# Where the bounds of q and k are formed, and how one planner prices its DMA queue: block-causal attention with a feed-forward layer

## The chip, the cores and the metric

The kernel runs on one core of one Trainium2 chip. The metric is the device time in microseconds. A core has TensorE (PE: matmuls, and weight loads shown as PEld), VectorE (DVE), ScalarE (ACT), GpSimd (POOL) and SyncE (SP), which here issues every load, store and DMA transpose from one queue in program order. Each engine runs its own instructions in the order in which they were written, and waits on semaphores for the others.

## The reference

```python
B, H, S, D = 8, 8, 576, 64
scores = (q @ k^T) / sqrt(D)              # mask: key block j <= query block i, blocks of 64
attn = exp(scores - rowmax); attn = attn / (sum(attn) + 1e-9)
x = (attn @ v) laid out as (B*S, H*D)     # 4608 tokens of 512
h = x @ w_in                              # 512 x 2048
g = h * clip(h + 3, 0, 6) / 6
out = g @ w_out                           # 2048 x 512, f32
```

All inputs and the output are f32.

## The kernel before

**Number format.** Most products are done in f16 with each operand split into a high and a low part (hi = round(a * scale), lo = a * scale - hi), and the partial products are summed in PSUM. The scale is a power of two, taken from an upper bound of the operand: `pow2_scale` sums a per-partition bound over the 128 partitions with a matmul by ones (tile `mb_q`), clears the mantissa (`pw_q`), divides and inverts (`rs_q`).

**Work units.** Heads are taken in pairs: 4 pairs for each of 8 batches, so 32 slots. The first batch (slots 0 to 3) is done in f32 by `qk_load32`, `qk_prep32`, `s_block32`, `t_block32` and `pv_group32`, so that it can start before any scale is known. Slots 4 to 31 are done in f16: `qk_load` (two DMA loads into `qk`), `qk_prep` (bound, scale, split into `qks`, DMA transpose into `qkT`), `s_group` (scores into PSUM tile `s`, row maxima, exp into `p`, normalised and split into `phl`, DMA transpose into `pT`), `pv_group` (attention times v, into the feed-forward's input `x`). The feed-forward goes over 13 pieces of up to 384 tokens; for each of 16 strips of 128 hidden columns `ffn1` makes `h`, ACT makes `r` = relu, DVE and ACT make `g`, and `ffn2` accumulates `o`. PSUM holds three `s` tiles, two `h` tiles and three `o` tiles. The weights are loaded, turned into f32 words and split during the first 180 us (`rawi`, `rawo`, `sgi`, `exi`, `win`, `wout`, and the bounds `abi`, `abo`, which ACT forms by Abs with a running sum).

**The order of the work** is not written by hand. A `Recorder` collects every operation with its operands, and `schedule` then plays them through a model of five engines: `cost` gives each instruction's time on its engine and its latency, and at each step an engine takes the ready operation with the lowest due time (`key`). The due times come from the constants at the top of the file: `AS`, `U`, `TA`, `PV0` for the f32 start, `RT` for the rest of batch 0, the table `AT` for slot starts, `FT` for the feed-forward, `S0`, `W0`, `M0` for the weights, `QL` for how many slot lengths ahead the loads of q and k are keyed. An operation added by `nc.scaled(..., "AV")` may go to ACT or DVE, whichever the model thinks ends first, with a bias against DVE; "P" adds POOL. The order that results is fixed for each engine when the program is built; on the chip only the waits move. In this model a DMA transpose has a fixed latency that does not depend on what else is in flight, and loads share a second, simple model of a queue.

**What the change touches.** In `qk_prep`, line 762 (`absmax(mx, t)`): one VectorE reduction with absolute values over 2 x 576 columns gives the bound of q and of k for each partition (tile `qkmx`). In `pv_group32`, lines 947 and 948: three small products on POOL fill `rd`, a diagonal of reciprocal row sums, which a matmul (tile `pr`) spreads for the f32 start, 12 times 3. In `s_group`, line 1033: VectorE multiplies the negated row maxima `st` by the scale `esc`, giving the bias of the exp. In `Recorder`: the pricing of DMAs at lines 208 to 218 and 423 to 426, and when a consumer counts as ready at line 438. Lines 26 to 53 and 81 hold the constants. `qks` has one buffer, `qk` two.

In the profile every recorded operation carries the line of `emit` (L452), so the groups are told apart by their tiles.

Of the kernel before, what the change touches and what calls it, by code (L numbers as in the profile page):

```python
# [9 lines left out]
BF16 = mybir.dt.bfloat16  # L10
# [3 lines left out]
AF = mybir.ActivationFunctionType  # L14
# [8 lines left out]
WX = 10  # L23
WY = 27

U = 2.788
AS = (7.494, 11.408, 15.3, 22.633)
AL = 14.807
PV0 = 2.519
TA, TR, PR = 2.197, 5.661, 0.677  # L30
QR = 3.417
PVA, PVB = 0.93, 1.25
PHS = 18
WLP = 0
WHA = 0
# [5 lines left out]
MEM = 0  # L41

NMIN = 64
QL = 0.849
VL = 0.2
W0, WD = 4.938, 2.891
S0, SD = 57.576, 4.59
M0, MD = 34.073, 5
RT = (25.619, 42.369, 59.881, 71.242)
RS, RL, VL1 = 2.796, 15.216, 24.0  # L50
VM0, VMX = 10.452, 0.3
AT = ((4, 86.25), (6, 128.63), (8, 159.32), (10, 199.92), (12, 240.31), (14, 287.79), (16, 335.13), (24, 565.96), (32, 826.62))
FT = ((0, 28), (1, 100), (2, 168.81), (3, 239.13), (4, 279.57), (5, 356.87), (7, 505.16), (10, 740.96), (13, 988.23))
QP = 0.55
VP = 0.5
BLK = 64
# [4 lines left out]
class Op:  # L61

    __slots__ = ("ways", "key", "preds", "joint", "n", "start", "end", "tiles", "eng", "half")


class Engine:
# [9 lines left out]
        return call  # L78


ADV = {("tensor", "a"): 60.0}


class Recorder:
# [3 lines left out]

    NAMES = ("tensor", "vector", "scalar", "gpsimd", "sync")
    LAT = {"tensor": 55, "vector": 37, "scalar": 39, "gpsimd": 65, "sync": 65}  # L90
    TURN = 95
    BIAS = {"vector": 250.0, "gpsimd": 500.0}
    EDGE = 0.0
# [66 lines left out]
    def add(self, ways):  # L160
        eng, method, args, kw = ways[0]
        outs, ins = self.operands(args, kw)
        last = self.ops[-1] if self.ops else None
        if eng == "tensor" and self.joint is not None and last and last.joint == self.joint:
            op = last
            calls, occ, _, _ = op.ways[eng]
            more, took, _ = self.cost(eng, method, args, kw, outs, ins)
            op.ways[eng] = (calls + [(method, args, kw)], occ + more, occ + took, False)
        else:
            op = Op()  # L170
            op.joint, op.n, op.ways = None, len(self.ops), {}
            for e, m, a, k in ways:
                op.ways[e] = ([(m, a, k)], *self.cost(e, m, a, k, *self.operands(a, k)))
            op.key = self.key - self.adv.get((eng, self.cls), 0.0)
            op.preds, op.tiles, op.start = {}, [], None
            op.half = eng == "tensor" and outs[0].ap[0][1] <= 64 and method == "matmul"
            if eng == "tensor":
                op.joint = self.joint
            self.ops.append(op)
        for a, w in [(a, False) for a in ins] + [(a, True) for a in outs]:  # L180
            if self.on_chip(a):
                self.touch(op, a, w)

    def touch(self, op, a, w):
# [17 lines left out]
        keep.append((op, w, p0, p1, b0, b1))  # L202
        self.hist[t.name] = keep

    def cost(self, eng, method, args, kw, outs, ins):


        n = self.count(outs[0])
        if method == "dma_start":
            nb = mybir.dt.size(outs[0].dtype)  # L210
            for _, c in list(outs[0].ap):
                nb *= c
            if kw.get("transpose"):
                occ = max(1290, 172 * nb / 32768 - 150)
                return occ, occ + (1100 if nb <= 4 * 32768 else 2100), False
            if eng == "gpsimd":
                return 1300, 2900 + nb / 170, False
            return 600, 2000 + nb / 170, False
        if eng == "vector":
            if method == "tensor_reduce":  # L220
                n = self.count(ins[0])
            else:
                ptr = any(isinstance(a, bass.AP) and self.count(a) == 1 for a in args[2:] if n > 1)
                ptr = ptr or n == 1 and method == "tensor_scalar_mul" and isinstance(args[2], bass.AP)
            wide = [a for a in ins if self.count(a) > 1 and not self.psum(a)]
            port = len(wide) > 1
            if method in ("tensor_scalar", "tensor_copy") and n > 1:
                if not any(self.psum(a) for a in outs + ins):
                    if len(outs[0].ap) == 2 or outs[0].ap[1][1] % 2 == 0:
                        n = n / (4 if mybir.dt.size(outs[0].dtype) + mybir.dt.size(ins[0].dtype) == 4 else 2)  # L230
                        port = True
            occ = 68 + 1.042 * n
            if method != "tensor_reduce" and ptr:
                occ += 57
            return occ, occ + 80, port
        if eng == "scalar":
            occ = 94 + 0.8335 * n
            if isinstance(kw.get("scale"), bass.AP):
                occ += 95
            if isinstance(kw.get("bias"), bass.AP):  # L240
                occ += 58
            if "accum_out" in kw:
                occ += 93
            return occ, occ + 105, False
        if eng == "gpsimd":
            if method == "memset":
                return 20 + 1.0 * n, 50 + n, False
            occ = 75 + (2.0 if method == "tensor_tensor" else 1.1) * n
            return occ, occ + 30, True
        f32 = mybir.dt.size(ins[0].dtype) == 4  # L250
        occ = max(n / 2.37, 26) * (4 if f32 else 1) + 2
        if f32 and method == "matmul":
            occ = max(occ, 200)
        if method == "transpose":
            occ = max(occ / 2, 100)
        if outs[0].ap[0][1] <= 64 and method == "matmul":
            occ = occ / 2
        return occ, occ + 172, False

    def schedule(self):  # L260
# [63 lines left out]
        while done < N:  # L324
# [95 lines left out]
            o.eng, o.start, o.end = e, t, t + took  # L420
            while head < N and ops[head].start is not None:
                head += 1
            if calls[0][0] == "dma_start" and not calls[0][2].get("transpose"):
                nb = (took - (2900.0 if e == "gpsimd" else 2000.0)) * 0.8
                dma = max(dma, o.end - nb - 400.0) + nb
                o.end = max(o.end, dma + 400.0)
            now[e] = t + occ
            self.busy[e] += occ
            for x in o.tiles:
# [5 lines left out]
            for s, flow in succ[pick]:  # L435
                rs = ready[s]
                for q in rs:
                    r = t if q == e and (e == "tensor" or not flow) else o.end + self.LAT[q]
                    rs[q] = max(rs[q], r)
                ndep[s] -= 1  # L440
                if not ndep[s]:
                    for q in rs:
                        heapq.heappush(pend[q], (rs[q], s))
# [12 lines left out]
def kernel(  # L456
# [92 lines left out]
    def absmax(o, i, axis=AX.XY):  # L549
        nc.vector.tensor_reduce(o, i, axis=axis, op=ALU.max, apply_absolute_value=True)  # L550
# [207 lines left out]
    def qk_prep(n):  # L758
        t = qn.pop(n)
        mx = sm.tile([P, 2], F32, tag="qkmx", name=f"qkmx{n}")  # L760
        sp = attp.tile([P, 3, NST, 2, D], F16, tag="qks", name=f"qks{n}", bufs=1)
        absmax(mx, t)
        pw, rs = pow2_scale(mx, 2, f"q{n}")
        sc = sm.tile([P, 2], F32, tag="esc", bufs=3, name=f"esc{n}")
        nc.vector.scalar_tensor_tensor(
            sc[:, 0:1], pw[:, 0:1], C_EXP, pw[:, 1:2], op0=ALU.mult, op1=ALU.mult
        )
        esc[n] = sc

        nc.scaled(sp[:, 0, :, 0], t[:, 0], rs[:, 0:1], "AV")  # L770
        nc.scaled(sp[:, 1, :, 0], t[:, 1], rs[:, 1:2], "AV")
        nc.vector.scalar_tensor_tensor(
            sp[:, 0, :, 1], t[:, 0], rs[:, 0:1], sp[:, 0, :, 0], op0=ALU.mult, op1=ALU.subtract
        )
        nc.vector.scalar_tensor_tensor(
            sp[:, 2, :, 0], t[:, 1], rs[:, 1:2], sp[:, 1, :, 0], op0=ALU.mult, op1=ALU.subtract
        )
        for c in (1, 2):
            nc.scaled(sp[:, c, :, 1], sp[:, c, :, 0], 1.0, "VPA")
        o = attp.tile([P, 3, 2 * S], F16, tag="qkT", name=f"qkT{n}")  # L780
        nc.sync.dma_start(
            o.rearrange("p c (t x) -> p (c t) x", x=P),
            sp.rearrange("p c t l d -> p (c t l d)"),
            transpose=True,
        )
        qkT[n] = o
# [153 lines left out]
    def pv_group32(n, g):  # L940
# [4 lines left out]
        nc.vector.reciprocal(r, r)  # L945
        rd = sm.tile([P, GB, BLK], F32, tag="rd", bufs=2, name=f"rd{n}_{g}")
        for i in range(GB):
            nc.gpsimd.tensor_scalar(rd[:, i], ident2, r[:, i:i + 1], 1.0, op0=ALU.mult, op1=ALU.mult)
        if g == 0 or PRO:
            o = 2 if g else len(n_ev) % 3  # L950
            pr = ps_o.tile([P, GT], F32, tag=f"o{o}", name=f"pr{n}_{g}")
# [36 lines left out]
    def s_group(n, g):  # L988
# [19 lines left out]
        for si, some in enumerate(banks):  # L1008
# [21 lines left out]
            i0, i1 = min(col[x[0]] for x in regions), max(col[x[0]] for x in regions) + 1  # L1030
            if len(some) > 1:
                nc.vector.tensor_tensor(st[:, 2:3], st[:, 2:3], st[:, 3:4], op=ALU.min)
            nc.vector.tensor_scalar_mul(st[:, 4 + i0:4 + i1], st[:, i0:i1], sc[:, 0:1])
            for ii, c0, c1, rg in regions:
                if ii not in prs:
                    prs[ii] = attp.tile([P, NJ * P], F32, tag="p", bufs=NPB, name=f"p{n}_{g * GB + ii}")
# [436 lines left out]
```

## Time and profile before

| | |
|---|---|
| time, median of 3 runs | 1059.81 us (1059.1 to 1061.09) |
| profiled execution, first to last instruction | 1063.1 us, mean granted clock 0.980; its device time is not listed apart from the span |
| instructions | 28968 |
| PE busy | 995.4 us (94%) |
| DVE busy | 833.9 us (78%) |
| ACT busy | 635.8 us (60%) |
| POOL busy | 75.9 us (7%) |
| DMA | 128.90 MB, 414199 packets, mean 121 GB/s |

The page gives busy times as shares of the span, the span in 40 slices of 26.6 us with one digit (tenths busy) for each, the clock granted to TensorE, and groups of instructions with the idle time ahead of them and what ended it. A clock of 0.50 means that TensorE ran at half speed.

### The profile page before, as it was taken

The page shows a single profiled execution, that of the slowest core. Times are in us where ns is not written, and L with a number is a line of the kernel's source. Part 1 is how long each engine was busy: PE and PEld are TensorE (multiplying, and loading weights), DVE is VectorE, ACT ScalarE, POOL GpSimd, SP SyncE. Part 2 cuts the span into 40 slices and gives each one's busy share as a digit, 9 for nine tenths or more (in the row PEclk, how much of TensorE's full clock was granted, in tenths as well). Part 3 has the DMA queues.
Part 4 walks back from the last instruction along what each step waited for, and adds up shares of the span by engine and source line. Part 5 has one row for each costly group of instructions (what it writes and reads, how often), then busy time and mean ns, then how long its engine had stood idle before and what let it go on. Part 6 is the DMA issues. An engine that isn't in the chain of part 4 may idle for free. (4 is left out here: it accounts for less than half of the span.)

```text
span 1063.1 us, 28968 instructions
## 1 busy us (share of the span) xinstructions
PE 995.4 (94%) x11588; PEld 726.0 (68%) x11588; DVE 833.9 (78%) x2308; ACT 635.8 (60%) x1548; POOL 75.9 (7%) x259
## 2 busy tenths in 40 slices
PE   6978967999999999999999999999999999999998
PEld 4645646776777867667766666777767777777776
DVE  4888999999999999899899889787898875332322
ACT  4668757666657676666776565566556563343332
POOL 3132220000000000000000000000000000000000
PEclk8998988999999999999999999999999999999999
DMA  6756546898889887888888779647656533000000
GB/s 157 189 166 180 141 111 140 140 185 156 152 159 171 153 152 143 147 164 149 156 143 181 133 116 167 118 77 143 117 90 128 92 80 57 1 31 2 31 1 31
DMA packets 414199, 128.90 MB, mean 121 GB/s; under 512 B 403184, under 2 KB 403440, under 8 KB 414064
## 3 DMA queue, kind: packets, MB, share of 16 engines
q1 hardware_dynamic: 414064, 127.05, 61.4%
q8 instruction: 91, 1.49, 0.6%
q14 instruction: 44, 0.36, 0.1%
HBM read 45.09 MB, written 9.44 MB: 51 GB/s over the span
## 5 line engine op out<-in xcount | busy, mean ns | idle before, releaser
L452 PE MATMUL h<-x,win 128*64 128x384 f16 (+2 forms) x4720 | 437.0, 321 | 1.8 <-DVE win L452 1.6
L452 PE MATMUL o<-wout,g 128*64 128x512 f16 (+3 forms) x3444 | 430.9, 381 | 2.2 <-DVE g L452 2.2
L452 PEld LDWEIGHTS <-win 128*64 128x64 f16 x4608 | 296.8, 110 | 69.9 <-issue 2.2
L452 PEld LDWEIGHTS <-g 128*64 128x64 f16 x3360 | 221.6, 110 | 105.9 <-issue 2.0
L452 ACT ACTIVATE r<-h,eg,sh 128x384 f32<-128x384 f32 (+1 forms) x240 | 137.1, 593 | 131.5 <-PE h L452 130.8
L452 ACT ACTIVATE p<-s,st,esc 128x64 f32<-128x64 f32 (+1 forms) x280 | 163.1, 587 | 73.6 <-DVE st L452 53.6
L452 DVE SCALAR_TENSOR_TENSOR r<-r,eg,h 128x384 f32<-128x384 f32 (+1 forms) x192 | 113.4, 592 | 116.1 <-ACT r L452 116.0
L452 DVE SCALAR_TENSOR_TENSOR phl<-p,st,phl 128x128 f16<-128x128 f32 (+4 forms) x252 | 135.3, 582 | 0.7 <-ACT phl L452 0.6
L452 ACT ACTIVATE g<-r 128x384 f16<-128x384 f32 (+1 forms) x165 | 84.5, 513 | 85.8 <-DVE r L452 84.9
L452 DVE SCALAR_TENSOR_TENSOR g<-r,g 128x384 f16<-128x384 f32 (+1 forms) x192 | 102.7, 535 | 29.9 <-ACT g L452 29.4
L452 DVE TENSOR_REDUCE st<-s 128x1 f32<-128x64 f32 (+1 forms) x280 | 120.0, 447 | 4.1 <-PE s L452 3.8
L452 PE MATMUL s<-qkT 128*64 128x64 f16 (+7 forms) x1120 | 99.0, 289 | 10.0 <-ACT p L452 6.4
L452 PEld LDWEIGHTS <-vhl 128*64 128x64 f16 x1680 | 72.3, 111 | 41.2 <-issue 25.3
L452 PE MATMUL pv<-pT,vhl 128*64 128x192 f16 (+2 forms) x1680 | 75.1, 235 | 24.8 <-DMA pT<-phl 20.8
L452 ACT ACTIVATE phl<-p,st 128x256 f16<-128x256 f32 (+4 forms) x135 | 70.4, 556 | 34.4 <-DVE st L452 18.7
L452 PEld LDWEIGHTS <-qkT 128*64 128x64 f16 x1120 | 60.0, 111 | 35.4 <-issue 13.0
L452 POOL MEMSET p<- 128x64 f32 x140 | 21.4, 154 | 521.4 <-DVE phl L452 492.5
L452 ACT ACTIVATION_READ_ACCUMULATOR p<-s,st,esc 128x1 f32 x280 | 55.1, 197 | 0.0
L452 DVE TENSOR_SCALAR phl<-p,st 128x512 f16<-128x512 f32 (+4 forms) x117 | 46.0, 424 | 1.8
L452 DVE SCALAR_TENSOR_TENSOR qks<-qk,rs_q,qks 128x576 f16<-128x576 f32 x56 | 44.7, 817 | 0.0
L452 ACT ACTIVATE x<-pv 128x192 f16<-128x192 f32 (+1 forms) x61 | 22.0, 360 | 33.4 <-PE pv L452 30.7
L452 DVE TENSOR_REDUCE qkmx<-qk 128x2 f32<-128x1152 f32 x28 | 37.6, 1344 | 1.6 <-DMA qk<-in_k_dram 1.6
(154 smaller groups left out, 819.4 us busy)
## 6 DMA issues: line engine op xcount, KB each, us to landing
out_dram<-osb SPq DMA_DIRECT2D x35, 256.0 KB, 2.5
vnat<-in_v_dram SPq DMA_DIRECT2D x64, 128.0 KB, 2.9
qk<-in_q_dram SPq DMA_DIRECT2D x28, 288.0 KB, 3.6
qk<-in_k_dram SPq DMA_DIRECT2D x28, 288.0 KB, 4.4
rawo<-in_moe_w_out_dram SPq DMA_DIRECT2D x15, 512.0 KB, 4.6
rawi<-in_moe_w_in_dram SPq DMA_DIRECT2D x14, 512.0 KB, 4.0
pT<-phl SPq DMA_TRANSPOSE x140, 3.4
vnat<-in_v_dram SPq DMA_DIRECT2D x32, 32.0 KB, 2.7
```

The lines of the kernel that those rows point to most:

```text
L452: getattr(eng, method)(*args, **kw)
```

## The change

It does five things. `qk_prep` forms the bounds of q and k by two ScalarE activations (Abs, with the running sum kept as `mx`), one for q and one for k, whose elementwise output goes to a part of `qks` that is overwritten afterwards; the VectorE reduction goes. `rd` is made on ACT or VectorE, not on POOL. The bias of the exp is made on ACT or VectorE, not on VectorE alone. The planner prices each DMA, transposes included, through one first-in-first-out queue (a lead, the bytes over a rate, a tail; three kinds), and a consumer on TensorE counts as ready 1.25 us after the planned landing; running sums on ACT get 195 ns of latency where they had 105. The constants of the due times are new (`VL` and `VM0` are read nowhere).

```diff
-U = 2.788
+U = 2.847
-AL = 14.807
-PV0 = 2.519
-TA, TR, PR = 2.197, 5.661, 0.677
-QR = 3.417
-PVA, PVB = 0.93, 1.25
+AL = 14.433
+PV0 = 2.291
+TA, TR, PR = 2.432, 5.661, 0.677
+QR = 2.99
+PVA, PVB = 0.879, 0.986
-QL = 0.849
-VL = 0.2
+QL = 1.341
+VL = -0.109
-S0, SD = 57.576, 4.59
+S0, SD = 55.147, 4.668
-RS, RL, VL1 = 2.796, 15.216, 24.0
-VM0, VMX = 10.452, 0.3
-AT = ((4, 86.25), (6, 128.63), (8, 159.32), (10, 199.92), ...
-FT = ((0, 28), (1, 100), (2, 168.81), (3, 239.13), ...
+RS, RL, VL1 = 2.796, 14.496, 24.609
+VM0, VMX = 11.693, 0.246
+AT = ((4, 86.25), (6, 128.63), (8, 159.32), (9, 178.32), (10, 199.92), ...
+FT = ((0, 28), (1, 100), (2, 165.7), (3, 239.13), ...
-ADV = {("tensor", "a"): 60.0}
+ADV = {("tensor", "a"): 61.31}
+    MARGIN = {"tensor": 1250.0}
+    QUEUE = {"load": (4137.0, -1860.0, 256.0), "store": (4137.0, -1860.0, 580.0), "turn": (4074.0, -2300.0, 182.0)}
@@ cost
-                occ = max(1290, 172 * nb / 32768 - 150)
+                occ = max(1290, 189 * nb / 32768 - 200)
             if "accum_out" in kw:
                 occ += 93
+                return occ, occ + 195, False
@@ schedule
-            if calls[0][0] == "dma_start" and not calls[0][2].get("transpose"):
-                nb = (took - (2900.0 if e == "gpsimd" else 2000.0)) * 0.8
-                dma = max(dma, o.end - nb - 400.0) + nb
-                o.end = max(o.end, dma + 400.0)
+            margin = {}
+            if o.queue:
+                lead, tail, work = o.queue
+                dma = max(t + lead, dma) + work
+                o.end = dma + tail
+                margin = self.MARGIN
-                    r = t if q == e and (e == "tensor" or not flow) else o.end + self.LAT[q]
+                    r = t if q == e and (e == "tensor" or not flow) else o.end + self.LAT[q] + margin.get(q, 0.0)
@@ qk_prep
-        absmax(mx, t)
+        for s in range(2):
+            ab = sp[:, 1 + s].rearrange("p t l d -> p (t l d)").bitcast(BF16)[:, :NST * D]
+            nc.scalar.activation(
+                ab.rearrange("p (t d) -> p t d", d=D), t[:, s], AF.Abs, accum_out=mx[:, s:s + 1]
+            )
@@ pv_group32
-            nc.gpsimd.tensor_scalar(rd[:, i], ident2, r[:, i:i + 1], 1.0, op0=ALU.mult, op1=ALU.mult)
+            nc.scaled(rd[:, i], ident2, r[:, i:i + 1], "AV")
@@ s_group
-            nc.vector.tensor_scalar_mul(st[:, 4 + i0:4 + i1], st[:, i0:i1], sc[:, 0:1])
+            nc.scaled(st[:, 4 + i0:4 + i1], st[:, i0:i1], sc[:, 0:1], "AV")
```

More of the change, by code (lines that the diff above doesn't have):

```diff
@@ L43 @@
 NMIN = 64
-QL = 0.849
-VL = 0.2
+QL = 1.341
+VL = -0.109
 W0, WD = 4.938, 2.891
-S0, SD = 57.576, 4.59
+S0, SD = 55.147, 4.668
 M0, MD = 34.073, 5
 RT = (25.619, 42.369, 59.881, 71.242)
-RS, RL, VL1 = 2.796, 15.216, 24.0
-VM0, VMX = 10.452, 0.3
-AT = ((4, 86.25), (6, 128.63), (8, 159.32), (10, 199.92), (12, 240.31), (14, 287.79), (16, 335.13), (24, 565.96), (32, 826.62))
-FT = ((0, 28), (1, 100), (2, 168.81), (3, 239.13), (4, 279.57), (5, 356.87), (7, 505.16), (10, 740.96), (13, 988.23))
+RS, RL, VL1 = 2.796, 14.496, 24.609
+VM0, VMX = 11.693, 0.246
+AT = ((4, 86.25), (6, 128.63), (8, 159.32), (9, 178.32), (10, 199.92), (12, 240.31), (14, 287.79), (16, 335.13), (24, 565.96), (32, 826.62))
+FT = ((0, 28), (1, 100), (2, 165.7), (3, 239.13), (4, 279.57), (5, 356.87), (7, 505.16), (10, 740.96), (13, 988.23))
 QP = 0.55
@@ L61 @@
 class Op:
-    __slots__ = ("ways", "key", "preds", "joint", "n", "start", "end", "tiles", "eng", "half")
+    __slots__ = ("ways", "key", "preds", "joint", "n", "start", "end", "tiles", "eng", "half", "queue")
 class Engine:
@@ L175, in add @@
             op.preds, op.tiles, op.start = {}, [], None
+            op.queue = self.queue(args, kw) if method == "dma_start" else None
             op.half = eng == "tensor" and outs[0].ap[0][1] <= 64 and method == "matmul"
@@ L203, in touch, with queue @@
         self.hist[t.name] = keep
+    def queue(self, args, kw):
+        nb = mybir.dt.size(args[0].dtype)
+        for _, c in list(args[0].ap):
+            nb *= c
+        kind = "turn" if kw.get("transpose") else "load" if self.on_chip(args[0]) else "store"
+        lead, tail, rate = self.QUEUE[kind]
+        return lead, tail, nb / rate
     def cost(self, eng, method, args, kw, outs, ins):
```

## The prediction

> **What bounds the kernel now.** First the head of the page and its slices: how much of the span TensorE works, and at what clock.
>
> ```profile
> span 1063.1 us, 28968 instructions
> PE 995.4 (94%) x11588; PEld 726.0 (68%) x11588; DVE 833.9 (78%) x2308; ACT 635.8 (60%) x1548; POOL 75.9 (7%) x259
> ...
> PE   6978967999999999999999999999999999999998
> DVE  4888999999999999899899889787898875332322
> PEclk8998988999999999999999999999999999999999
> ```
>
> TensorE is busy nearly everywhere, and its last 160 us are feed-forward alone, with DVE at 2 to 3 tenths. So there is always a backlog for TensorE: a microsecond in which it idles or runs at half clock, wherever it is, comes back at the end of the span. The stages, by windows (columns: length, then PE, PEld, DVE, ACT, POOL busy, clock, DMA share, GB/s):
>
> ```profile
> 0.00:186.00 186.00, 151.91 (x974) 98.88 (x976) 156.10 (x421) 127.89 (x344) 47.43 (x103) 0.91 0.61 155
> 186.00:580.00 394.00, 375.82 (x5092) 279.80 (x5090) 373.66 (x1104) 267.80 (x663) 17.82 (x98) 1.00 0.87 157
> 580.00:895.00 315.00, 303.37 (x3771) 223.57 (x3768) 254.97 (x700) 182.47 (x437) 10.62 (x58) 0.99 0.62 113
> 895.00:1063.10 168.10, 164.28 (x1762) 123.75 (x1758) 49.16 (x85) 57.63 (x106) 0.00 (x0) 1.00 0.04 15
> ```
>
> Subtracting PE busy, the idle time is 34.1, 18.2, 11.6 and 3.8 us, 67.7 in all. DVE is 95% busy (373.66 of 394) in the second stage, DMA 0.87. Next, whom TensorE waited for, from the waits of 0 to 240 us and then of 186 to 895 us (us in total, times, longest):
>
> ```profile
> PE pr L452 <- POOL rd L452: 8.3, 5, 2.9
> PE pt L452 <- ACT pf L452: 8.3, 6, 6.1
> PE s L452 <- ACT p L452: 3.3, 1, 3.3
> ```
>
> ```profile
> PE pv L452 <- DMA pT<-phl: 20.8, 20, 2.5
> PE s L452 <- ACT p L452: 3.1, 5, 1.6
> ```
>
> From 186 on, 20.8 of 29.8 us of idle time end with the transpose of the probabilities; ahead of that, POOL's `rd` and late softmax pieces. Each long gap, in the timeline, and behind it the stretches at half clock, by windows:
>
> ```profile
> 60.57 0.59 PE L452 MATMUL pr<-rd,halves 128*128 128x192 f32 x2 [2.93 <-POOL rd L452]
> 79.47 1.01 PE L452 MATMUL pr<-rd,halves 128*128 128x192 f32 x2 [2.68 <-POOL rd L452]
> 143.13 0.47 PE L452 MATMUL pt<-ident,pf 128*128 128x128 f32 x1 [6.13 <-ACT pf L452]
> 171.04 0.85 PE L452 MATMUL s<-qkT 128*64 128x64 f16 x12 [3.31 <-ACT p L452]
> 436.91 1.07 PE L452 MATMUL pv<-pT,vhl 128*64 128x192 f16 x18 [2.03 <-DMA pT<-phl]
> 586.77 0.85 PE L452 MATMUL pv<-pT,vhl 128*64 128x192 f16 x18 [2.52 <-DMA pT<-phl]
> ```
>
> ```profile
> 61.94:65.35 3.41, 3.41 (x13) 2.33 (x12) 2.49 (x6) 2.87 (x9) 0.15 (x1) 0.50 0.13 13
> 79.01:89.25 10.24, 7.44 (x20) 5.07 (x21) 7.65 (x20) 7.20 (x18) 3.47 (x7) 0.50 0.37 107
> 140.45:147.27 6.82, 3.78 (x17) 3.08 (x18) 6.11 (x19) 3.54 (x11) 0.49 (x3) 0.50 0.24 77
> 167.75:174.58 6.83, 3.54 (x42) 3.10 (x43) 6.83 (x24) 5.62 (x13) 1.23 (x2) 0.50 0.71 142
> 437.41:440.82 3.41, 3.41 (x28) 1.82 (x24) 2.56 (x7) 1.53 (x6) 0.30 (x2) 0.50 0.70 131
> 587.59:591.00 3.41, 3.41 (x24) 1.52 (x22) 2.38 (x10) 0.33 (x1) 0.15 (x1) 0.50 0.90 166
> ```
>
> Every one of the six gaps has a stretch at clock 0.50 at it or right behind it. Work done there would take half as long at full clock, so such a stretch costs half its PE busy time: 1.7, 3.7, 1.9, 1.8, 1.7 and 1.7 us, 12.5 in all. A gap of 2 us thus costs nearly 4.
>
> The Trainium skill (TensorE: Matmul & The Clock Gate, Part 1) says that the clock halves after at least one idle window of about 3.4 us. By that page only the 6.13 us gap would be followed by half speed, and removing the two `pv` gaps would bring 1.7 us each less than I count. The gaps of 2.03 and 2.52 us above disagree, so the trace decides.
>
> **The change, part by part.** The prices:
>
> ```profile
> L452 DVE TENSOR_REDUCE qkmx<-qk 128x2 f32<-128x1152 f32 x28 | 37.6, 1344 | 1.6 <-DMA qk<-in_k_dram 1.6
> L452 ACT ACTIVATE abi<-win 128x512 f32<-128x512 f32 x14 | 8.7, 624 | 3.7 <-DVE win L452 3.2 <-DVE rsio L452 0.2
> L452 ACT ACTIVATION_READ_ACCUMULATOR abi<-win 128x1 f32 x14 | 2.7, 189 | 0.0
> L452 DVE TENSOR_SCALAR st<-st,esc x168: 184/208/586, 146.5 to 880.2; 128x1 f32<-128x1 f32 x112, 128x3 f32<-128x3 f32 x28, 128x2 f32<-128x2 f32 x28
> L452 DVE TENSOR_SCALAR phl<-p,st 128x128 f16<-128x128 f32 x21 | 5.7, 289 | 0.6
> L452 POOL TENSOR_SCALAR rd<-ident,sums 128x64 f32<-128x64 f32 x36 | 18.4, 530 | 37.1 <-DVE sums L452 25.3 <-DVE pw_v L452 11.6 <-DVE am_q L452 0.2
> 56.62 3.89 POOL L452 TENSOR_SCALAR rd<-ident,sums 128x64 f32<-128x64 f32 x3 [1.16 <-DVE sums L452]
> 76.40 3.01 POOL L452 TENSOR_SCALAR rd<-ident,sums 128x64 f32<-128x64 f32 x3 [0.84 <-DVE sums L452]
> ```
>
> *1. `rd` off POOL.* On DVE one costs between 0.208 us (the median for one to three columns) and 0.289 (128 columns), say 0.25, so 0.75 for three. The two groups that took 3.89 and 3.01 us on POOL would end 3.1 and 2.3 us earlier, which covers the gaps of 2.93 and 2.68 but for about 0.4 us. All `pr` waits gone would give 8.3 us, and the half clocks at 61.94 and 79.01 another 5.4: 13.7 at best. Against it stand 36 x 0.25 = 9 us more on DVE or ACT, in a stage where DVE is 84% busy (156.10 of 186); if all of that reached TensorE and nothing were won, +9. The third and fourth gap show what is late next there: a softmax piece behind DVE. I take a little under half of the best, -6.
>
> *2. Margin and one DMA queue.* For pv the planner waits 1.25 us longer after the planned landing and fills in feed-forward work, of which there is a backlog. The mean wait is 20.8/20 = 1.04 us, so by itself the margin covers most; at best all 20.8 and the two half clocks of 1.7, or -24.2. But the margin shifts a plan, and the lateness comes from DVE and the DMA queue drifting away from the plan: moved transposes meet other loads, which are now keyed about half a slot earlier on the same SP queue, and stand ahead of transposes there. If that merely moved the waits, 0; if every transpose met one more load, each of 20 waits could grow by as much as it is now, +20.8. I take half of 20.8 and two thirds of the clock, -12. The feed-forward that `pv` delays has work ahead of it, which hides the margin's own 1.25 us; without backlog the margin would cost 20 x 1.25 = 25.
>
> *3. 37.6 us less on DVE.* In the second stage its worth lies in step 2 (the late `phl`) and is not counted again. In the first, four of the reductions stand between 114.6 and 181.5 us:
>
> ```profile
> L452 DVE TENSOR_REDUCE qkmx<-qk x4: 1341/1342/1346, 114.6 to 181.5; 128x2 f32<-128x1152 f32 x4
> L452 DVE TENSOR_REDUCE qkmx<-qk x16: 1334/1344/1354, 218.1 to 555.2; 128x2 f32<-128x1152 f32 x16
> L452 DVE TENSOR_REDUCE qkmx<-qk x8: 1341/1343/1354, 579.0 to 787.1; 128x2 f32<-128x1152 f32 x8
> ```
>
> There DVE is full, and the gaps of 6.13 and 3.31 us end behind it. At best 4 x 1.34 + 3.7 of clock (rows 140.45 and 167.75) = -9.1; at worst 0. DVE gets part of `rd` instead: -2.
>
> *4. Two Abs on ACT, 28 times.* 576 columns against 512: 0.624 x 576/512 = 0.70, plus 0.19 for reading the sum, 0.89 each, 28 x 1.78 = 50 us more on ACT, from about 115 to 790 us. ACT is 68% busy in the second stage (267.80 of 394); its 16 slots add 28 us, 75%. What can reach TensorE: its waits for ACT are 3.1 us of 450 us of ACT work from 186 on (under 1%, 0.3 us for the new 50), and 8.3 + 3.3 of 127.89 in the first stage (9%, 4.5 us). The upper end is all 50, the lower end 0, since no row shows a gain from a longer ACT queue. Since `r`, `p` and `g` queue behind each Abs in order, I take more than the average row, +6. Behind `mx` stand `mb_q`, the scales, `qks` and the transpose: the bound comes 1.78 us after start where it came after 1.34, 0.4 later, hidden by a slot of (787 - 114.6)/27 = 25 us. Abs writes into the single `qks`, so it must wait for the transpose before; the same 25 us hide that. Without that cover it would cost the whole wait, 28 times.
>
> *5. Bias on either.* 168 products, at 0.208 us by the row above; if half go to ACT, 17 us move from DVE to ACT. ACT's price lies between 0.19 (the read of a sum) and 0.62 (512 columns); nearer the first, some 0.3, so +25 us on ACT. With the exp next on the same engine one crossing goes. Both directions are as small as the average shares of step 4 (below 1 us): 0, with ends of -3 and +3.
>
> *6. New due times.* They redraw the whole order. Of the 34.1 us idle in the first stage 34.1 - 8.3 - 6.1 - 3.3 = 16.4 have no part of the change aimed at them; half of it may go or come again: 0, ends -8 and +8.
>
> Sum: -6 - 12 - 2 + 6 + 0 + 0 = -14. Against the profiled span that is 1063.1 - 14 = 1049.1; the median of the runs stands 3.3 us below the span, so 1059.81 - 14 = 1046.
>
> **The rivals.**
>
> *A larger gain.* Steps 1 to 3 come near their ends and ACT's burden stays at the average: -10 - 20 - 4 + 2 = -32, or 1028. For it: TensorE's backlog; against it: DMA at 0.87 and DVE still near 90% (373.66 - 16 x 1.34 = 352 of 394).
>
> *The waits only move.* TensorE has an order that was fitted to the old plan; a new plan has new mistakes, and the biggest gap, 6.13 us, is itself one. Then steps 1 and 2 keep a quarter (-5), ACT takes its +6: 1061, and between 1054 and 1062.
>
> *Slower: Abs ahead of relu.* ACT runs in order, and there are two `h` tiles: an Abs pair of 1.78 us in front of `r` holds an `h` tile, and TensorE stands. The price is 50 us if all reaches TensorE; against -20 from the other steps it decides from 40% on. At two thirds: 33 - 20 = +13, or 1073. Against it: from 186 on TensorE waited 3.1 us for ACT's exp, and no row has it waiting for `r`. The Trainium skill (ScalarE: Activation LUTs, Rules for kernel authors) sends maxima to VectorE and not to ScalarE, which speaks for this rival; the rows agree as far as engine time goes (1.78 against 1.34), but the rule does not ask which engine is full.
>
> **How the numbers follow.** The forecast, 1040 to 1054, gets 0.50; the larger gain (1028 to 1040) 0.13; moved waits 0.22, of which 0.12 still below 1057.7 and 0.10 within; slower 0.15. About 0.2% (2.1 us, so 1057.7 to 1061.9) is what a measurement of this kernel tells from no change. Faster: 0.50 + 0.13 + 0.12 = 0.75; same 0.10; slower 0.15. The range leaves out the slower rival and the last 0.05 of the large gain: 1033 to 1062.
>
> **What the next profile shows.** Step 1: no wait for `rd` of over 1 us, and clock 1.00 from about 55 to 95 us. Step 2: waits of `pv` for `pT` at 8 to 12 us in total, none over 2. Step 3: DVE about 30 us less busy, no `qkmx` reduction. Step 4: ACT 50 to 75 us busier, Abs at 0.70, and TensorE's waits for ACT up by less than 8 us. The forecast fails if TensorE's idle time from 186 on stays near 30 us (plan and chip still apart), or if waits for `r` or `p` appear in place of `pT`.

## The result, and the profile after

The changed kernel takes 1026.09 us (median of 4 runs, 1025.1 to 1030.27) against 1060.45 us (1059.1 to 1065.02, 4 runs) for the kernel before: a ratio of 0.967, 95% interval 0.963 to 0.971. It is 34 us faster where 14 were forecast, 7 us below the lower end of the stated range. Its time came out where the rival "a larger gain" (1028) stood, though not for that rival's reasons. Ratios of different sets of runs should be compared with care: the median of the kernel before was between 1060 and 1068 us from set to set.

The head of the page of the changed kernel, and its slices, as they were shown of before:

```profile
span 1023.3 us, 29007 instructions
PE 988.6 (97%) x11588; PEld 720.9 (70%) x11588; DVE 796.0 (78%) x2191; ACT 694.1 (68%) x1783; POOL 61.3 (6%) x225
...
PE   6999888999999999999999999999999999999998
DVE  5899999999999899989999888787787874232322
PEclk9899998999999999999999999999999999999999
```

The stages of the changed kernel, by windows (length, then PE, PEld, DVE, ACT, POOL busy, clock, DMA share, GB/s):

```profile
0.00:186.00 186.00, 164.76 (x1142) 107.98 (x1144) 162.80 (x462) 146.88 (x412) 33.80 (x72) 0.94 0.67 165
186.00:580.00 394.00, 386.01 (x5258) 287.87 (x5256) 366.30 (x1071) 310.07 (x822) 18.64 (x104) 1.00 0.94 164
580.00:895.00 315.00, 313.32 (x3866) 232.05 (x3864) 229.81 (x597) 191.97 (x466) 8.89 (x49) 1.00 0.55 98
895.00:1023.30 128.30, 124.52 (x1332) 92.96 (x1328) 37.09 (x64) 45.22 (x84) 0.00 (x0) 0.99 0.06 20
```

TensorE's idle time is now 21.2, 8.0, 1.7 and 3.8 us where it was 34.1, 18.2, 11.6 and 3.8. Together with 6.8 us less PE busy time (995.4 to 988.6, for the same 11588 matmuls) that is the whole difference of the profiled spans: 12.9 + 10.2 + 9.9 + 6.8 = 39.8 = 1063.1 - 1023.3. Most of the lower busy time is clock: the stretches at half speed add up to 23.9 us (the three windows of the second block), where they were 41.0 us (the six of the prediction and the first row below, a seventh). TensorE worked 20.1 us in them where it had worked 31.2, and half of that difference is 5.5 of the 6.8 us.

```profile
20.98:27.81 6.83, 6.19 (x24) 3.70 (x24) 1.97 (x5) 2.76 (x9) 0.28 (x1) 0.50 0.94 290
```

```profile
21.60:35.25 13.65, 12.42 (x47) 8.03 (x47) 7.92 (x24) 6.97 (x22) 0.00 (x0) 0.50 0.80 218
130.80:134.21 3.41, 3.41 (x18) 3.06 (x17) 3.29 (x14) 3.37 (x10) 0.30 (x2) 0.51 0.46 137
154.70:161.53 6.83, 4.29 (x47) 3.63 (x47) 6.83 (x23) 6.12 (x15) 1.22 (x2) 0.50 0.69 140
```

Whom TensorE waits for in the changed kernel, over the whole span (us in total, times, longest):

```profile
...
PE s L467 <- ACT p L467: 2.9, 3, 2.5
PE pv L467 <- ACT p L467: 2.8, 5, 1.7
...
PE pr L467 <- ACT rd L467: 2.4, 3, 1.5
...
PE pv L467 <- DMA pT<-phl: 0.3, 1, 0.3
```

The 20 waits of `pv` for the transposed probabilities, 20.8 us before, have become one of 0.3. The transposes themselves did not get faster. From issue to landing they take (first before, then after; us):

```profile
DMA to landing us min/median/max: 3.0/3.4/6.8
```

```profile
DMA to landing us min/median/max: 3.0/4.1/6.6
```

So TensorE's order now asks for the data when it is there. The prices forecast for the moved work were right: an Abs over 576 columns takes 0.678 us and 0.194 for its sum (0.87 together, 0.89 forecast), a bias on ACT 0.29 (0.3 forecast).

```profile
L467 ACT ACTIVATE qks<-qk 128x576 bf16<-128x576 f32 x56 | 37.7, 678 | 6.0 <-DMA qkT<-qks 5.8
L467 ACT ACTIVATION_READ_ACCUMULATOR qks<-qk 128x1 f32 x56 | 10.8, 194 | 0.0
L467 ACT ACTIVATE st<-st,esc 128x1 f32<-128x1 f32 x79 | 22.8, 289 | 25.9 <-DVE st L467 25.4
```

### The profile page after: what moved, and what is told of

Its sections match the earlier page's. It is cut to its first block, busy times and chain, and to the rows that moved or that the text cites. A ratio compares the mean times of both kernels' runs of the same rounds, so it can differ in the third digit from the quotient of the medians.

```text
span 1023.3 us, 29007 instructions
## 1 busy us (share of the span) xinstructions
PE 988.6 (97%) x11588; PEld 720.9 (70%) x11588; DVE 796.0 (78%) x2191; ACT 694.1 (68%) x1783; POOL 61.3 (6%) x225
## 5 line engine op out<-in xcount | busy, mean ns | idle before, releaser
L467 PE MATMUL o<-wout,g 128*64 128x512 f16 (+2 forms) x3444 | 427.5, 378 | 0.3 <-DVE g L467 0.3
L467 PEld LDWEIGHTS <-g 128*64 128x64 f16 x3360 | 219.4, 110 | 105.2
L467 ACT ACTIVATE g<-r 128x384 f16<-128x384 f32 (+1 forms) x149 | 75.6, 508 | 78.5 <-DVE r L467 78.1
L467 DVE TENSOR_REDUCE st<-s 128x1 f32<-128x64 f32 (+1 forms) x280 | 116.3, 447 | 3.4 <-PE s L467 3.4
L467 PE MATMUL s<-qkT 128*64 128x64 f16 (+7 forms) x1120 | 96.8, 289 | 6.6 <-ACT p L467 2.9
L467 ACT ACTIVATE phl<-p,st 128x256 f16<-128x256 f32 (+4 forms) x123 | 66.1, 566 | 23.8 <-DVE st L467 13.5
L467 ACT ACTIVATE st<-st,esc 128x1 f32<-128x1 f32 (+2 forms) x123 | 35.7, 291 | 51.5 <-DVE st L467 50.7
L467 POOL MEMSET p<- 128x64 f32 x140 | 21.2, 151 | 558.7 <-DVE phl L467 525.8
L467 DVE TENSOR_SCALAR phl<-p,st 128x384 f16<-128x384 f32 (+4 forms) x129 | 49.7, 417 | 3.2
L467 ACT ACTIVATE qks<-qk 128x576 bf16<-128x576 f32 x56 | 37.7, 678 | 6.0 <-DMA qkT<-qks 5.8
```

The lines of the kernel that those rows point to most:

```text
L467: getattr(eng, method)(*args, **kw)
```

## The experiments

The theories: (1) the planner's new pricing of DMAs removed the waits; (2) the relief of DVE did; (3) the new due times, or a lucky order, did.

**The change split in two.** Only the three moves between engines, on the kernel before:

```diff
 # kernel before
-        absmax(mx, t)
+        two Abs activations on ACT, as in the change
-            nc.gpsimd.tensor_scalar(rd[:, i], ...)
+            nc.scaled(rd[:, i], ident2, r[:, i:i + 1], "AV")
-            nc.vector.tensor_scalar_mul(st[:, 4 + i0:4 + i1], ...)
+            nc.scaled(st[:, 4 + i0:4 + i1], ..., "AV")
```

> The kernel before with only the three moves between engines (Abs on ACT, rd and the bias on either); the planner's prices and the due times are those of before. Theory 1 (the planner's pricing of DMAs removed the waits for pT): 1048 to 1054 us, waits of pv for pT still 15 us or more, only the waits for rd gone. Theory 2 (a less loaded DVE makes phl early enough): 1028 to 1038 us, waits for pT under 5 us. Theory 3 (the due times): 1055 us or more.

Measured: ratio 1.0024 (1.0004 to 1.0045), 1069.3 us, slightly slower. That is also short of the 1048 to 1054 us of theory 1, which still counted `rd`'s gain, and it fits the time that theory 3 named. The profiled execution (span 1076.3 us) is the longest of eleven. The waits for the transposes stay (TensorE's waits from 186 us on):

```profile
PE pv L452 <- DMA pT<-phl: 23.7, 19, 2.8
PE s L452 <- DMA qkT<-qks: 6.3, 6, 1.6
```

DVE was 347.56 us busy from 186 to 580 us where it was 373.66, and TensorE waited as before. That refutes theory 2: the relief of DVE does not by itself remove the waits. Only the pricing:

```diff
 # changed kernel: the three moves undone, all due-time constants of before;
 # QUEUE, MARGIN, the rate of a transpose, the latency of a running sum stay
```

> The kernel before with only the planner's new pricing (one queue for all DMAs, the margin of 1.25 us, the new transposing rate, the longer latency of a running sum); no engine moves, due times of before. Theory 1: waits for pT under 3 us, 1034 to 1042 us. Theory 2: waits for pT still above 12 us, 1050 us or more. Theory 3: 1055 us or more.

Measured: ratio 0.9687 (0.9659 to 0.9716), 1033.8 us. Its interval overlaps that of the changed kernel (0.963 to 0.971), and DVE is as busy as before (834.5 us, 833.9 before). The head of its page, its stages and its wait for the transposes:

```profile
span 1029.0 us, 28978 instructions
PE 989.0 (96%) x11588; PEld 734.4 (71%) x11588; DVE 834.5 (81%) x2326; ACT 628.5 (61%) x1529; POOL 75.1 (7%) x260
```

```profile
0.00:186.00 186.00, 156.34 (x1047) 101.46 (x1049) 162.43 (x442) 131.29 (x352) 47.54 (x106) 0.94 0.62 157
186.00:580.00 394.00, 388.72 (x5251) 296.64 (x5248) 385.48 (x1148) 262.36 (x651) 17.80 (x99) 1.00 0.90 160
580.00:895.00 315.00, 313.75 (x3906) 238.24 (x3903) 247.89 (x672) 188.12 (x440) 9.75 (x55) 1.00 0.58 108
```

```profile
PE pv L467 <- DMA pT<-phl: 0.3, 1, 0.3
```

From 186 to 895 us TensorE idles 5.3 + 1.2 = 6.5 us instead of 29.8, although DVE is 98% busy (385.48 of 394). So a DVE that is nearly full did not hold TensorE up here, once the plan had the DMA landings right. The waits for POOL's `rd` fell too, from 8.3 to 1.7 us, and the clock is full from 55 to 95 us, although `rd` is still made on POOL (TensorE's waits of 0 to 186 us, and the window):

```profile
PE pr L467 <- POOL rd L467: 1.7, 4, 0.7
```

```profile
55.00:95.00 40.00, 37.28 (x226) 22.98 (x222) 37.38 (x92) 32.91 (x85) 15.73 (x21) 1.00 0.69 197
```

**The due times.** The changed kernel with all due-time constants of before:

> The changed kernel with all constants of the due times as before. Theory 3: most of the gain is gone, 1045 us or more. Theories 1 and 2: within 8 us of the changed kernel, 1026 to 1034 us, the difference in the first 186 us.

Measured: ratio 0.9645 (0.9619 to 0.967), 1028.8 us. The new constants are without a visible effect; theory 3's first half falls. This kernel and the pricing alone (1033.8 us, the same set of runs) differ by the three moves only, and no run of the one overlaps a run of the other (1027.4 to 1030.3 against 1030.8 to 1035.2). So with the moves it came out 5 us faster there, 0.5%, where on the kernel before they lost 0.24%. Orders that differ by a nudge alone lie up to 0.45% apart (see the controls), so a gain of the moves is not shown.

**Queue against margin.** Three kernels: the changed kernel without the margin, the pricing alone without the margin, and the kernel before with nothing but a margin.

```diff
 # no_margin: changed kernel; queue_only: the kernel "pricing"
-    MARGIN = {"tensor": 1250.0}
+    MARGIN = {}
 # margin_only: kernel before
                     r = t if q == e and (...) else o.end + self.LAT[q]
+                    if q == "tensor" and calls[0][0] == "dma_start":
+                        r += 1250.0
```

> The changed kernel without the 1.25 us of margin; the queue stays. If the margin is what removes the waits: waits for pT back at 8 to 15 us, 1036 to 1045 us. If the fitted queue by itself places the transposes well enough: waits under 3 us, 1024 to 1030 us. By theory 2 too it stays within 5 us of the changed kernel.

> The kernel before with the planner's one queue, the new transposing rate and the longer latency of a running sum, without the margin; no engine moves, due times of before. By analogy with the changed kernel without margin (9.9 us of waits for pT): waits of 8 to 14 us, ratio 0.976 to 0.986. If the queue were all that counts: waits under 3 us, ratio 0.970 or less. If the margin were: ratio 0.99 or more.

> The kernel before with one line more in the planner: a consumer on TensorE counts as ready 1.25 us after the planned landing of a DMA. No queue, no engine moves, due times of before. If the margin does most: waits for pT 4 us or less (the 20 waits of before, each 1.25 us shorter), ratio 0.975 to 0.982. If the queue is needed to place the transposes: waits of 8 us or more, ratio 0.985 or more.

Measured: without the margin 0.9765 (0.9731 to 0.98); queue alone 0.9825 (0.979 to 0.986); margin alone 0.984 (0.9809 to 0.9871). The waits of `pv` for the transposes from 186 us on, in that order:

```profile
PE pv L467 <- DMA pT<-phl: 9.9, 13, 1.9
```

```profile
PE pv L467 <- DMA pT<-phl: 10.7, 15, 2.1
```

```profile
PE pv L454 <- DMA pT<-phl: 5.8, 10, 1.2
```

On the kernel before, with the pricing's other small parts counted to the queue, the four corners are 1 (20.8 us of waits), 0.984 (margin, 5.8), 0.9825 (queue, 10.7) and 0.9687 (both, 0.3; from another set of runs): the two gains nearly add up, 1.6% and 1.75% against 3.1% for both. Neither part replaces the other. The queue alone leaves waits of up to 2.1 us (2.5 before) and halves their sum; the margin alone leaves ten of up to 1.2 us, a little more than was expected of it (5.8 us for 4 or less, and 0.984 for 0.975 to 0.982).

The queue is not simply a longer latency. For a transpose of n blocks of 128 x 128 f16 that finds the queue empty, the plan before counted 172 n - 150 ns, at least 1290, and 2100 more; the new one counts 4074 - 2300 + 180 n ns. For the smallest `pT` transposes (8 blocks) that is 3.39 and 3.21 us, for the largest (18) 5.05 and 5.01, so nearly the same. What differs is what stands ahead of it.

**Twice the margin**, 2.5 us, in the changed kernel:

> The changed kernel with twice the margin, 2.5 us. If a backlog of feed-forward work hides the margin: no more waits for pT, ratio within 0.4% of the changed kernel's 0.967, so 0.963 to 0.971. If the margin itself costs TensorE time for want of work: 0.975 or more.

Measured: ratio 0.9648 (0.9618 to 0.9678), 1026.6 us. No wait for the transposes is left in the list, and in this order the larger margin costs nothing: the backlog hides it.

**Controls.** One due-time constant nudged, in the kernel before (60.0 to 61.31) and in the changed one (61.31 to 60.0):

> The kernel before with one due-time constant nudged (the lead of the attention's TensorE work, 60.0 to 61.31), which redraws the order and does nothing else. It measures how much a new order by itself moves the time. Theory 1: ratio within 0.994 to 1.006, waits for pT still 15 us or more. If a lucky order explains the gain: a change of 1% or more.

> The changed kernel with the one due-time constant nudged back (61.31 to 60.0), a control that redraws the order only. Within 0.3% of the changed kernel's 0.967 if the new order is robust; waits for pT under 1.5 us. How far it lies from the changed kernel is what the three others have to be measured against.

Measured: 0.9977 (0.9944 to 1.001) with 17.7 us of waits for the transposes from 186 us on, and 0.9627 (0.96 to 0.9654) with 0.2.

```profile
PE pv L452 <- DMA pT<-phl: 17.7, 19, 1.8
```

```profile
PE pv L467 <- DMA pT<-phl: 0.2, 1, 0.2
```

A new order by itself neither makes nor unmakes the gain. But the second control lies 0.45% below the changed kernel's 0.967 from another set, more than the 0.3% expected, so a few tenths of a per cent between two orders prove nothing.

**Each move undone by itself**, in the changed kernel, in the same set of runs as the control at 0.9627: the bounds on VectorE, `rd` on POOL, the bias on VectorE.

> The changed kernel with the bounds of q and k as maxima on VectorE again; everything else as changed. DVE about 37 us busier than in the changed kernel, ACT about 49 us less. If the bounds on ACT pay: a ratio 0.3% or more above the changed kernel's 0.967. If ACT's longer queue cost about what DVE's relief gave: within 0.3% of it. The prediction's own steps 3 and 4 make the move a loss of 4 us: ratio about 0.963.

> The changed kernel with rd on POOL again. The prediction's step 1 gives 6 us to the move: ratio about 0.973, waits for rd of 5 us or more and a half-clock stretch behind one of them. If the new order hides POOL's delay: within 0.3% of the changed kernel.

> The changed kernel with the bias of the exp on VectorE alone. ACT about 36 us less busy (123 products of 0.29 us), DVE about 25 us more. The prediction's step 5 says no difference: within 0.3% of the changed kernel. If the bias on ACT shortens the softmax's chain: slower by 0.5% or more.

Measured: 0.9618 (0.9591 to 0.9646), 0.9694 (0.9661 to 0.9727) and 0.9608 (0.9581 to 0.9636). Where the bounds and the bias are made has no effect on the time that these runs show. With the bounds on VectorE DVE is busy 816.3 us, only 20 more than in the changed kernel and not the 37 expected, and ACT 674.8 us, 19 less and not 49: the planner moves other work the opposite way. `rd` on POOL is slower by 0.7% (7.2 us) than the control, which is about the 6 us of step 1. These waits stand in its first 186 us:

```profile
PE pr L467 <- POOL rd L467: 4.9, 5, 2.0
PE h L467 <- DVE r L467: 4.8, 1, 4.8
```

Only 2.5 us of it lie at `rd` itself: TensorE waited 4.9 us for it, and in the control 2.4. The other wait, for `r`, ends at 165.29, 22 us behind the last wait for `rd`.

**`rd` by itself**, on the kernel before and on the pricing alone:

> The kernel before with rd on ACT or DVE and nothing else changed. By the prediction's step 1 (6 us): ratio 0.992 to 0.996, no wait for rd over 1 us, clock full from 55 to 95 us. If the move pays only in an order whose other waits are gone: within 0.2% of 1.

> The kernel before with the new pricing and rd's move; bounds and bias on VectorE, due times of before. If the rest of the change is without effect: the changed kernel's ratio, 0.960 to 0.967, some 0.4 to 0.7% below pricing alone (0.969).

Measured: 1.0007 (0.9987 to 1.0027), and 0.9715 (0.968 to 0.975), against 0.9687 for the pricing without it in another set. Both miss what was expected: no gain of the move shows in either. In the first of these the waits for POOL are gone (one of 1.4 us for an `rd` made on ACT remains), and others stand near their place (timeline):

```profile
55.30 1.12 PE L452 MATMUL o<-wout,g 128*128 128x512 f32 x2 [2.26 <-DVE g L452]
82.50 2.08 PE L452 MATMUL o<-wout,g 128*128 128x512 f32 x2 [2.52 <-DVE g L452]
143.17 0.48 PE L452 MATMUL pt<-ident,pf 128*128 128x128 f32 x1 [6.46 <-ACT pf L452]
```

So on the kernel before TensorE was held up there by more than `rd`, and the next wait shows when the first is taken away. On the pricing alone there was little left to gain: the new order had already closed those gaps with `rd` on POOL (1.7 us of waits). Why `rd` on POOL costs 0.7% in the changed kernel is not settled, since orders differ by some tenths of a per cent anyway.

**Two attempts at a faster kernel.** The changed kernel with bounds and bias on VectorE and a margin of 2.5 us; and the changed kernel with the due times of before and a margin of 2.5 us.

> The changed kernel with the bounds and the bias on VectorE again and a margin of 2.5 us: only the parts that paid, with the larger margin. By the separate runs (each within 0.3% of the changed kernel): ratio 0.959 to 0.965. If DVE becomes the bound with all of its work back: 0.968 or more.

> The changed kernel with the due times of before and a margin of 2.5 us. Each by itself was level with the changed kernel or a little better (0.9645 and 0.9648): ratio 0.958 to 0.966.

Measured: 0.9703 (0.9667 to 0.9738), 1031.95 us, and 0.9706 (0.967 to 0.9741), 1031.65 us. Both miss what was expected, and neither beats the changed kernel. The second differs from the kernel with the due times of before (0.9645) by its margin alone and comes out 0.6% higher, in another set of runs; so the larger margin is not shown to be free in every order. No variant could be told from the changed kernel to the good.

## Why the prediction was wrong

The direction and the frame held: TensorE with a backlog, so that each idle or half-clocked microsecond comes back at the end. The sum failed in one large term; smaller ones were off in both directions.

*Step 2 is the term that failed: -12 forecast, about -34 measured in the profiled span of the pricing alone* (1063.1 to 1029.0; ratio 0.9687). I counted only half of the 20.8 us of waits, on the ground that the rest would merely move. They did not move: the margin by itself took out 15.0 us of them, the queue by itself 10.1, and both together 20.5. With the queue alone the waits that are left are mostly below 1.25 us (15 of 0.7 us on average, the longest 2.1), which the margin covers. Of the 34 us, 23.3 are idle time from 186 us on (29.8 to 6.5), the 20.5 among them; 4.4 are idle time of the first stage (34.1 to 29.7); and 6.4 are PE busy time (995.4 to 989.0), while the stretches at half speed shrank from 41.0 to 20.5 us. My bound of -24.2 was no bound: it counted only the waits of one kind and the two half-clock stretches behind them, and nothing for the first stage, where the new order shortened waits and half-speed stretches too. The further load that I feared for each transpose is there in the changed kernel: the DMA share of the second stage rose from 0.87 to 0.94 and the median landing from 3.4 to 4.1 us (0.90 and 3.5 with the pricing alone). No wait came of it.

*Step 1, -6 for `rd`: not shown.* By itself the move closed the two gaps, as its arithmetic had it, but DVE's `g` came late near the same place, 2.26 and 2.52 us (`rd` alone: 1.0007). I had written that something else, a softmax piece, would be late next, and still counted 6 us. The new pricing closed the same gaps without the move, so the gains of steps 1 and 2 could not be added. Only undoing the move in the changed kernel cost about the forecast (7.2 us), and 2.5 us of that stand at `rd`.

*Step 3, -2, and step 4, +6: together nothing that shows* (bounds back on VectorE: 0.9618 against 0.9627); whether each is nothing or they cancel, this run cannot tell. The durations were right, their sum was not. A likely reason is that the planner rebalances the work that may go to either engine. The 4.5 us of step 4 also took the first stage's share of 9% for all 50 us, where only four of the 28 slots lie; 7 us at 9% would be 0.6. Signs that were named for steps 1, 3 and 4 came true without a gain that shows: the clock is full from 55 to 95 us, DVE is 37.9 us less busy and ACT 58.3 us more. One cover that step 4 named was not there: Abs does wait for the transpose that still reads the single `qks`, although slots are 25 us apart. In the kernel with only the moves ACT stood 16.2 us for it, in the changed one 5.8:

```profile
L452 ACT ACTIVATE qks<-qk 128x576 bf16<-128x576 f32 x56 | 37.9, 678 | 16.2 <-DMA qkT<-qks 16.2
```

That may be why the moves alone lost 0.24%; it was not tried apart.

*Steps 5 and 6, 0 and 0: right* (0.9608 against 0.9627; due times of before 0.9645). 123 of the 168 biases went to ACT, where I had assumed half.

*The rivals.* "A larger gain" had the time but shared it over steps 1 to 3. "The waits only move" is what happened to `rd` alone, on the kernel before. "Abs ahead of relu" did not come: the bounds on ACT cost nothing measurable. So the Trainium skill's advice to keep maxima off ScalarE (ScalarE: Activation LUTs, Rules for kernel authors) made no difference here, in either direction, where a sum of absolute values stood in for the maximum.

## What to carry to other kernels

Where the bounding engine has a backlog and runs in a fixed order, as here, look at its idle time first as error of the plan and not as lack of work: find whose landing the plan has wrong, and correct that price, before moving work between engines. Here a fitted queue took out half of such waits, a safety margin nearly three quarters, and both nearly all (20.8 us to 10.7, 5.8 and 0.3); the margin was free where other work could fill it (2.5 us in the changed kernel), though one other order was slower with 2.5 us. Do not halve a gain on the ground that waits will merely move without a row that shows where to; for a wait that a single chain causes, do look for the next late member of that chain.

## What the runs showed of the hardware

Half speed does not follow every gap of 2 us. Before, a gap of 2.03 us was followed by clock 0.50. With `rd` alone one of 2.26 us (ending at 55.30) was not, and one of 2.52 (ending at 82.50) lies in such a stretch:

```profile
53.04:60.00 6.96, 4.44 (x23) 2.56 (x23) 6.96 (x15) 6.24 (x16) 1.28 (x2) 1.00 0.54 151
...
80.60:87.40 6.80, 4.90 (x19) 2.73 (x20) 4.68 (x9) 5.20 (x13) 1.36 (x2) 0.51 0.38 133
```

In the changed kernel 13.65 us at half speed, from 21.60 on, contain no gap over 1.45 us:

```profile
22.61 1.01 PE L467 MATMUL pr<-rd,halves 128*128 128x192 f32 x2 [1.45 <-ACT rd L467]
```

The stretches last 3.41, 6.83, 10.24 and 13.65 us, multiples of one length. Cut by that length, back from where a stretch begins, the time ahead of it gives windows whose busy time can be compared. The first row is the window ahead of 437.40 before. The next two are with `rd` alone: the window ahead of 80.75, and the one eight lengths earlier, which holds most of the gap of 2.26 us. The last is the window ahead of 21.61 in the changed kernel:

```profile
433.99:437.40 3.41, 1.38 (x19) 0.75 (x20) 3.41 (x11) 1.35 (x2) 0.31 (x1) 1.00 0.44 86
...
77.34:80.75 3.41, 1.51 (x6) 0.92 (x6) 3.41 (x12) 3.29 (x11) 0.53 (x1) 1.00 0.73 216
...
53.44:56.86 3.42, 1.56 (x7) 1.04 (x8) 3.42 (x7) 2.94 (x10) 0.93 (x1) 1.00 0.67 170
...
18.20:21.61 3.41, 1.74 (x7) 0.74 (x6) 3.38 (x13) 3.04 (x14) 0.00 (x0) 1.00 1.09 252
```

TensorE was busy 1.38 and 1.51 us in the first two windows, and half speed followed; it was busy 1.56 us in the third, and none followed. So the share of idle time in such a window seems to count, rather than the longest gap. But the fourth, with 1.74 us, was followed by half speed as well, so the share alone does not settle it. This is read from these rows, not tested.
